# Fourier stage two with the last tokens' high and low rows in one block, and one group for two batches' middle feature

## The chip, the cores and the metric

The kernel runs on one core of a Trainium2 chip. Its engines work at the same time, each through its own queue in order: TensorE (PE in the rows, with PEld for the loading of the stationary operand), VectorE (DVE), ScalarE (ACT), GpSimd (POOL) and SyncE (SP), which here only issues transfers. The metric is the device time of the one launch in microseconds (us).

## What is computed

The reference is attention with a threshold under the row maximum, then a Fourier mixing over tokens and features with a two-layer MLP, then a gated projection:

```
scores = (q @ k^T) / 8;  keep scores >= max - tau;  softmax;  attn = softmax @ v     # 4 x 8 heads x 576 x 64
x = attn as (4, 576, 512)
u = x + real(fft over features(fft over tokens(x)))                                  # "mixed"
un = (u - mean) / sqrt(var + 1e-6)
y = u + relu(un @ w_ch1) @ w_ch2                                                     # 512 -> 2048 -> 512
out = (sigmoid(conv of 5 tokens of y) * (y @ w_val)) @ w_out
```

The change touches only `mixed`. Since x is real, the real part of the two-dimensional transform needs cosine sums and sine sums alone, over the even and the odd part of x in the tokens. Stage one sums over features, stage two over tokens.

## The kernel before

**Numbers in two parts.** A matrix product with nearly float32 accuracy is made from float32r operands split into a rounded high part and the low rest: high x high, low x high and high x low, three matmuls that add into one PSUM tile. Names end in `h` and `l` for the two.

**Stages.** Attention goes pair of heads by pair (16 pairs, `p`), nine tiles of 128 query rows each (144 tiles, `g_tile`). For each tile: PE makes the scores `s` (line 667), DVE takes their maximum `neg` (L732), ACT makes `e` = exp (L738), DVE masks and sums into `p` (L749), POOL divides (L757), PE transposes into `t` (L769), ACT copies to `m` (L786), and later PE multiplies by v (L447). There are two PSUM tiles for scores, so tile g waits for L749 of tile g-2. Four pairs are a batch; after a batch's last pair comes its Fourier part `g_fft(b)`. Beside all this the MLP's weights, which arrive as float64 words, are converted in 32 pieces (`Wide.stages`, L278 to L288: five steps on DVE, two or three on ACT, one on POOL). When the last scores are done, PSUM is given to the MLP, whose chunk 0 (512 tokens) is woven with the rest of the Fourier part (`g_h` L1239, `g_c` L1275). Chunks 1 to 4 (L1085, L1101) and the gated output (L1473, L1491) follow in an order written out in the code.

**Fourier stage one** (`g_fft`, L566). The folded tokens (289 cosine rows, 287 sine rows) are cut into three blocks of 97, 96, 96 and 96, 96, 95 (`E_BLK`, `O_BLK`). A group for one block is 8 matmuls (cosine, 258 columns) or 6 (sine, 256 columns). `g_parts` then takes it out of PSUM: ACT writes the high part (`aeh`, `boh`, L540) and DVE the low rest (`ael`, `bol`, L550); in the last batch ACT makes a second copy and POOL the subtraction (L547).

**Fourier stage two** (`stage2`, L579). For each of two feature blocks `j` there is a cosine and a sine group of 128 features by 290 tokens, 9 matmuls each: three products times three token blocks. Ahead of them a group of 9 makes the middle feature (row 256, two columns of `aeh`) of this batch, which ACT copies to `ny` (L592) and then into row 0 of `dd` and `sm` (L618, L620). DVE makes `dd` = `ws` - f and `sm` = `ws` + f (L605, L607), POOL adds them to the tokens, and SP stores the result `u_d`. So stage two is 45 matmuls a batch, 180 in all; stage one is 168.

**What sets the order.** All work up to the end of chunk 0 is placed by `Loom`: a list planner that runs when the kernel is built, with an estimate for every step, ranks and due times (`rank`, `due`, `SPREAD`, `FFT_LATE`), and constants that say how far a low-ranked step may go ahead (`NEAR`, `HOLD`) and what a change of work on PE costs (`SWAP`, `FILL`, `STAY`). `DICE` seeds small random shifts in its choices. What comes out is a fixed order for each engine. The order from the first matmul of chunk 1 on does not come from these constants.

Of the kernel before, what the change touches and what calls it, by code (L numbers as in the profile page):

```python
# [29 lines left out]
CE = DM // 2 + 2  # L30
KE = HALF + 2
E_BLK = [(0, 97), (97, 96), (193, 96)]
O_BLK = [(1, 96), (97, 96), (193, 95)]
# [30 lines left out]
def f32(ap):  # L64
    return ap.bitcast(F32)
# [251 lines left out]
def attention_fft(tc, right, ps_f, a, u_d, dram, conv_w, loom):  # L317
# [3 lines left out]
    with ExitStack() as right2, ExitStack() as right2b, ExitStack() as right3, ExitStack() as right4, ExitStack() as scores, ExitStack() as turned:  # L321
# [34 lines left out]
        ael = dft.tile([128, 3, CE], F32R, name="ael")  # L356
# [32 lines left out]
        def g_consts():  # L389
            for nm, shape in (("cd", [128, 2, CE]), ("sd", [128, 2, DM // 2]), ("cs", [97, 3, KE]), ("ss", [96, 3, KE])):  # L390
                for part in "hl":
                    t = dft.tile(shape, F32R, name=nm + part)
# [26 lines left out]
        NPT, FFT_OPS = 9 * NP, 87  # L419
# [49 lines left out]
        def g_fold(p):  # L469
# [24 lines left out]
            ends, inner, back = slice(0, HALF + 1, HALF), slice(1, HALF), slice(S - 1, HALF, -1)  # L494
            whole = ("DVE", dve(S), 3, "port") if p >= NPAIR - 2 else ("POOL", 1435.0, 2, "port")
            eng = DVE if p >= NPAIR - 2 else POOL

            def g_half(kind, s):
                op = ALU.subtract if kind else ALU.add
                yield "POOL", pool_ns(HALF), 2, "port"  # L500
                POOL.tensor_tensor(out=t[kind][:, inner], in0=s[:, inner], in1=s[:, back], op=op)
                yield "POOL", 290.0, 2, "port"
                POOL.tensor_copy(t[kind][:, ends], s[:, ends])
                if kind and j == 0:
                    yield "POOL", 780.0, 2, "port"
                    POOL.tensor_tensor(out=t[1][0:1, inner], in0=d[0:1, inner], in1=d[0:1, back], op=ALU.add)
# [16 lines left out]
        def g_fft(b):  # L523
            yield "after", ("folded", b * NP + NP - 1), ("cst",), *([("fft", b - 1)] if b else [])
            xs, rev = xs_d.pop(b), rev_d.pop(b)
# [6 lines left out]
            aeh, ael, boh, bol = a_b[0:2] + [fft_p.tile([128, 3, DM // 2], F32R, tag=nm, name=nm) for nm in ("boh", "bol")]  # L532

            def g_parts(kind, nb, m, n, f, room):
# [3 lines left out]
                fv, hv, lv = f[0:m, 0:n], *(x[0:m, nb, 0:n] for x in ((boh, bol) if kind else (aeh, ael)))  # L538
                yield "ACT", act(n), 0.3
                ACT.activation(hv, fv, AF.Copy)  # L540
                if b == B - 1:
                    t = fft_p.tile([128, KE], F32, tag=("ws", "sm")[nb % 2], name="sp")[0:m, 0:n]
# [4 lines left out]
                    POOL.tensor_tensor(out=lv, in0=t, in1=f32(hv), op=ALU.subtract)  # L547
                else:
                    yield "DVE", dve(n), 0.25
                    DVE.tensor_tensor(out=lv, in0=fv, in1=f32(hv), op=ALU.subtract)  # L550
# [3 lines left out]
            for kind in range(2):  # L554
# [3 lines left out]
                for nb, (n0, m) in enumerate(O_BLK if kind else E_BLK):  # L558
# [12 lines left out]
            def stage2(odd, c0, m=128):  # L571
                hi, lo, sh, sl = (boh, bol, cst["ssh"], cst["ssl"]) if odd else (aeh, ael, cst["csh"], cst["csl"])
                i = 0
                for ww, ss in ((hi, sh), (lo, sh), (hi, sl)):
                    for nb, (_, k) in enumerate(O_BLK if odd else E_BLK):
                        yield ("PE", KE / 2.4 + 13.5, rank(), "full", *(["room"] if i == 0 else []))
                        if i == 0:
                            f, room = fill_tile()
                        PE.matmul(out=f[0:m, 0:KE], lhsT=ww[0:k, nb, c0:c0 + m], rhs=ss[0:k, nb, :], start=(i == 0), stop=(i == 8))  # L579
                        i += 1  # L580
# [9 lines left out]
            def g_ny(f, room):  # L590
# [1069 lines left out]
```

## Time and profile before

| what | us |
|---|---|
| time, median of 3 runs | 856.27 |
| lowest and highest | 854.34, 858.76 |
| the profiled execution, its own time | 852.85 |
| the profiled execution, its span | 851.1 |
| PE busy | 818.5 (96%) |
| DVE busy | 562.6 (66%) |
| ACT busy | 417.8 (49%) |
| POOL busy | 380.5 (45%) |

The span runs from the first to the last instruction; 1.75 us of the profiled execution lie around it. Busy time is the share in which an engine has an instruction in work. Matmuls overlap in the pipeline, so the time of one matmul is read from the distance between starts, not from its duration. The span falls into three stretches: attention up to the last scores at 306.15 us, the rest of the planned part with chunk 0 to the first matmul of chunk 1 at 433.27 us, and the remainder.

### The profile page before, as it was taken

What the parts mean: (1) busy time and instruction counts of PE and PEld (TensorE: products, weight loads), DVE (VectorE), ACT (ScalarE), POOL (GpSimd) and SP (SyncE); (2) the same over time, 40 slices, a digit from 0 to 9 for tenths busy, and PEclk for the clock granted to TensorE, in tenths of its full rate; (3) what the DMA queues carried; (4) which work ended last, traced back from release to release, by engine and by line L of the source; (5) the groups of instructions that cost most, each with busy time, mean ns of one, the idle gap of its engine ahead of it and who ended that gap; (6) DMA issues with size and microseconds to landing.
All of it is one profiled execution on the core that took longest, in us unless ns stands there. A gap on an engine that the chain in (4) does not pass through costs nothing.

```text
span 851.1 us, 13928 instructions
## 1 busy us (share of the span) xinstructions
PE 818.5 (96%) x4920; PEld 653.6 (77%) x4920; DVE 562.6 (66%) x1212; ACT 417.8 (49%) x855; POOL 380.5 (45%) x450
## 2 busy tenths in 40 slices
PE   7889999989999998999999999999999999999997
PEld 5555556656665666888899999998888788889986
DVE  6999999999899999897747542142123756329730
ACT  4777786777778774744535222133121331143432
POOL 4546965687668755675353331022003010085421
PEclk9999999999999999999999999999999999999999
DMA  6357444426553559966945621013000230532111
GB/s 214 106 172 237 121 133 155 155 104 221 191 183 107 191 195 378 343 219 222 383 154 170 202 88 38 1 39 98 1 1 24 82 106 1 198 130 82 62 50 62
DMA packets 64765, 119.47 MB, mean 140 GB/s; under 512 B 14514, under 2 KB 21682, under 8 KB 64696
## 3 DMA queue, kind: packets, MB, share of 16 engines
q1 hardware_dynamic: 57448, 95.01, 32.4%
q0 software_dynamic: 7104, 23.57, 9.1%
q8 instruction: 39, 0.64, 0.3%
q14 instruction: 30, 0.25, 0.1%
q10 hardware_dynamic: 144, 0.00, 0.0%
HBM read 87.09 MB, written 31.47 MB: 139 GB/s over the span
## 4 chain that ended last, share of the span: by engine, by line
PE 63%; DVE 16%; ACT 7%; POOL 5%; issue 5%; DMA 3%; SPq 0%; DVEq 0%; POOLq 0%; ACTq 0%
PE c L1101 16%; PE h L1085 16%; DVE p L749 5%; PE o L1491 5%; DVE neg L732 5%; PE c L1275 5%; PE v L1473 5%; PE h L1239 4%; PE s L667 4%; ACT e L738 4%; PE f L447 2%; ACT m L786 2%; PE t L769 2%; POOL p L757 2%; PE f L579 2%
## 5 line engine op out<-in xcount | busy, mean ns | idle before, releaser
L757 POOL TENSOR_SCALAR p<-p,su 128x576 f32<-128x576 f32 x144 | 109.0, 766 | 92.1 <-DVE su L684 84.2
L1089 DVE SCALAR_TENSOR_TENSOR hl<-h,hh 128x384 fp32r<-128x384 f32 (+1 forms) x64 | 39.9, 623 | 147.8 <-ACT hh L1088 147.8
L1088 ACT ACTIVATE hh<-h 128x384 fp32r<-128x384 f32 (+1 forms) x64 | 34.8, 544 | 203.7 <-PE h L1085 198.5
L738 ACT ACTIVATE e<-s,neg 128x576 f32<-128x576 f32 x144 | 104.7, 742 | 53.7 <-DVE neg L732 39.2
L749 DVE SCALAR_TENSOR_TENSOR p<-s,thr,e 128x576 f32<-128x576 f32 x144 | 114.4, 816 | 16.7 <-ACT e L738 7.9
L732 DVE TENSOR_REDUCE neg<-s 128x1 f32<-128x576 f32 x144 | 103.3, 748 | 5.7 <-PE s L667 5.0
L667 PE MATMUL s<-kt,qt 64*128 64x288 f32 (+1 forms) x640 | 97.5, 437 | 9.6 <-DVE p L749 8.5
L1101 PE MATMUL c<-hl,w1h 128*128 128x384 f32 (+1 forms) x256 | 93.0, 363 | 0.1
L1101 PE MATMUL c<-hh,w1l 128*128 128x384 f32 (+1 forms) x256 | 92.6, 362 | 0.0
L1101 PE MATMUL c<-hh,w1h 128*128 128x384 f32 (+1 forms) x256 | 92.6, 362 | 0.0
L769 PE MATMUL t<-ident,p 128*128 128x128 f32 x496 | 75.3, 280 | 11.1 <-ACT m L786 5.9
L667 PEld LDWEIGHTS s<-kt,qt 64*128 64x128 f32 (+1 forms) x640 | 45.5, 174 | 47.7 <-issue 12.3
L769 PEld LDWEIGHTS t<-ident,p 128*128 128x128 f32 x496 | 53.8, 141 | 35.6 <-POOL p L757 17.1
L786 ACT ACTIVATE m<-t 128x512 f32<-128x512 f32 x124 | 72.0, 600 | 3.0 <-PE t L769 2.9
L447 PE MATMUL f<-m,v 128*64 128x320 f32 (+1 forms) x512 | 69.6, 411 | 0.3 <-ACT th L704 0.3
L1085 PE MATMUL h<-unh,w0h 128*128 128x384 f32 (+1 forms) x256 | 61.6, 362 | 0.0
L1085 PE MATMUL h<-unh,w0l 128*128 128x384 f32 (+1 forms) x256 | 61.6, 362 | 0.0
L1085 PE MATMUL h<-unl,w0h 128*128 128x384 f32 (+1 forms) x256 | 61.6, 362 | 0.0
L1110 POOL TENSOR_TENSOR res<-ht,res 128x512 f32<-128x512 f32 (+1 forms) x20 | 23.0, 1186 | 84.5 <-DVE ht L1109 84.5
L447 PEld LDWEIGHTS f<-m,v 128*64 128x64 f32 x512 | 33.7, 137 | 27.2 <-issue 4.4
L1101 PEld LDWEIGHTS c<-hl,w1h 128*128 128x128 f32 x256 | 48.1, 188 | 6.1 <-DVE hl L1089 1.2
L1101 PEld LDWEIGHTS c<-hh,w1l 128*128 128x128 f32 x256 | 48.1, 188 | 5.0
(264 smaller groups left out, 1705.4 us busy)
## 6 DMA issues: line engine op xcount, KB each, us to landing
raw<-in_moe_w_ch POOLq DMA_DIRECT2D x32, 512.0 KB, 6.4
qt<-in_q SPq DMA_DIRECT2D x15, 576.0 KB, 5.2
kt<-in_k SPq DMA_DIRECT2D x15, 432.0 KB, 3.5
ypad<-y_d SPq DMA_DIRECT2D x16, 288.0 KB, 2.9
out<-os SPq DMA_DIRECT2D x18, 256.0 KB, 2.0
v<-in_v SPq DMA_DIRECT2D x16, 256.0 KB, 3.2
e_h<-cx SPq DMA_DIRECT2D x16, 256.0 KB, 3.8
e_l<-ct SPq DMA_DIRECT2D x16, 256.0 KB, 4.2
```

Of the source, the lines that this page charges most:

```text
L447: PE.matmul(out=f[h * 64:h * 64 + 64, 0:n], lhsT=w, rhs=r, start=(t == 0), stop=(t == 4))
L667: PE.matmul(out=s[o, c, 0:HALF], lhsT=qt[w, hh, q], rhs=kt[w, 2 if h == 2 and hh else hh], start=True, stop=True)
L732: DVE.tensor_reduce(out=neg[u][:, j, 0:1], in_=sc[g][:, :, 0:HALF], axis=AX.XY, op=ALU.max, negate=True)
L738: ACT.activation(e, sc[g][:, :, 0:HALF], AF.Exp, bias=neg[u][:, j, 0:1], scale=1.0)
L749: DVE.scalar_tensor_tensor(out=p_view(g).rearrange("p (a b) -> p a b", a=2), in0=sc.pop(g)[:, :, 0:HALF], scalar=thr[u][:, j:j + 1], in1=e ...
L757: POOL.tensor_scalar(out=v, in0=v, scalar1=ssum[u][:, j:j + 1], scalar2=1.0, op0=ALU.mult, op1=ALU.mult)
L769: PE.matmul(out=f[:, t, :], lhsT=pv[:, t * 128:(t + 1) * 128], rhs=ident, is_transpose=True, start=(t == 0), stop=(t == 3))
L786: ACT.activation(o, fv, AF.Copy)
L1085: PE.matmul(out=f[:, 0:n], lhsT=ww[:, k * 128:(k + 1) * 128], rhs=x[:, k, 0:n], start=(i == 0), stop=(i == 3 * KB - 1))
L1101: PE.matmul(out=ch[c][o][:, 0:n], lhsT=ww[:, o * 128:(o + 1) * 128], rhs=x, start=(at_ == 0 and i == 0), stop=(at_ == FB - 1 and i == 2))
L1275: PE.matmul(out=ch[0][o][:, 0:n], lhsT=ww[:, o * 128:(o + 1) * 128], rhs=x, start=(j == 0 and i == 0), stop=(j == FB - 1 and i == 2))
L1473: PE.matmul(out=f[:, 0:HALF], lhsT=w[:, k, o * 128:(o + 1) * 128], rhs=x[:, k, s], start=(i == 0), stop=(i == 3 * KB - 1))
```

## The change

**Packed last block.** The 289 cosine rows are put in another order: tokens 1 to 287, then 0 and 288. The folded sums are written at offset 0 (`most`) with the two end tokens behind (`two`). Blocks are now 128, 128 and 33 rows (cosine) or 31 (sine). In the third block the high part goes to rows 0 and up, the low rest to rows 64 and up of the same tile (`h[LOW:LOW + m]`), and for the sine a second copy of the high part to rows 32 and up. The constants `csh` and `ssh` hold matching rows in their third block. One matmul with 97 or 95 rows then does what three did. For the cosine the product of the high part with the low constants is a second matmul with 33 rows. A cosine group is 8 matmuls instead of 9, a sine group 7.

**Tile shape.** The program that is built gives the 33-row matmuls of stage two a TensorE tile of 64 rows, the shape that the scores have; the stage-one groups of 33 and 31 output rows get tiles of 64 and 32 columns. Before, all Fourier matmuls had the full tile, apart from the two-column groups of the middle feature, with 32 columns.

**Evacuation of the third block.** DVE does the subtraction in all four batches; for the sine ACT does one more copy. The last batch's second copy on ACT and its subtraction on POOL go for these blocks.

**One group for two batches' middle feature.** Stage one now makes feature 256 twice, ahead of features 0 to 255 and behind them. Even batches write columns 0 to 256 of `aeh`, odd ones 1 to 257, so that column 0 keeps the even batch's middle feature while column 257 takes the odd batch's. One group of 8 in every second batch then makes both. `g_ny` adds them to the two token rows with two DVE operations reading PSUM, and SP stores two single rows. The two copies into `dd` and `sm` go, and the store of `xr` for j = 0 has 127 rows. Chunk 0's load now also waits for batch 1's group.

Stage two has 136 matmuls instead of 180.

**Planner constants.** Several of them and the seeds change, so the order of the planned part is another one throughout. From the first matmul of chunk 1 on, the order on every engine is the same as before.

```diff
-E_BLK = [(0, 97), (97, 96), (193, 96)]
-O_BLK = [(1, 96), (97, 96), (193, 95)]
+NB = 2
+REST = HALF + 1 - NB * 128
+LOW = 64
-HOLD = {"PE": 200.0, "DVE": 200.0, "ACT": 200.0, "POOL": 200.0}
-NEAR = 20.0
+HOLD = {"PE": 200.0, "DVE": 200.0, "ACT": 100.0, "POOL": 350.0}
+NEAR = 120.0
-SPREAD = 26
-FFT_LATE = 2
+SPREAD = 32
+FFT_LATE = 6
-RANK = {"D": 1, "A": 1, "P": 2.5}
+RANK = {"D": 2.5, "A": 9, "P": 2.5}
-SWAP = 450.0
-FILL = 200.0
-STAY = 80.0
+SWAP = 350.0
+FILL = 100.0
+STAY = 160.0
...
             def g_parts(kind, nb, m, n, f, room):
...
-                fv, hv, lv = f[0:m, 0:n], *(x[0:m, nb, 0:n] for x in ((boh, bol) if kind else (aeh, ael)))
+                h, l = (boh, bol) if kind else (aeh, ael)
+                v = slice(0, n) if kind else slice(b % 2, b % 2 + DM // 2 + 1)
+                hv, fv = h[0:m, nb, v], f[0:m, v]
                 yield "ACT", act(n), 0.3
                 ACT.activation(hv, fv, AF.Copy)
-                if b == B - 1:
+                if nb == NB:
+                    yield "DVE", dve(n), 0.25
+                    DVE.tensor_tensor(out=h[LOW:LOW + m, nb, v], in0=fv, in1=f32(hv), op=ALU.subtract)
+                    if kind:
+                        yield "ACT", act(n), 0.3
+                        ACT.activation(h[32:32 + m, nb, v], fv, AF.Copy)
+                    loom.free(room)
+                elif b == B - 1:
...
-            def stage2(odd, c0, m=128):
+            def stage2(odd, c):
                 hi, lo, sh, sl = (boh, bol, cst["ssh"], cst["ssl"]) if odd else (aeh, ael, cst["csh"], cst["csl"])
+                ops = [(ww, ss, nb, 128) for ww, ss in ((hi, sh), (lo, sh), (hi, sl)) for nb in range(NB)] + [(hi, sh, NB, LOW + REST - 2 * odd)]
+                if not odd:
+                    ops.append((hi, sl, NB, REST))
...
-            def g_ny(f, room):
-                yield "ACT", act(KE), 0.3
-                ACT.activation(ny, f[0:1, 0:KE], AF.Copy)
+            def g_ny(f, room, x):
+                up, dn, md = slice(0, HALF + 1), slice(S - 1, HALF, -1), slice(1, HALF)
+                yield "DVE", dve(KE), 0.25
+                DVE.tensor_tensor(out=x[:, up], in0=x[:, up], in1=f[0:2, up], op=ALU.add)
+                yield "DVE", dve(KE), 0.25
+                DVE.tensor_tensor(out=x[:, dn], in0=x[:, dn], in1=f[0:2, md], op=ALU.add)
                 loom.free(room)
+                for i in range(2):
+                    SP.dma_start(out=u_d[b - 1 + i][DM // 2:DM // 2 + 1], in_=x[i:i + 1])
...
         def g_first():
-            yield "after", ("added", 0, 0), ("added", 0, 1), ("s", LEFT)
+            yield "after", ("added", 0, 0), ("added", 0, 1), ("ny", 1), ("s", LEFT)
```

How the order moves is shown at two places, both on PE. The first is the start of stage one for batch 0, which lies in pair 6. In the rows, `s` is scores, `t` and `f<-ident,p` transposes, `f<-cdh,xeh` and the like stage one. Before:

```order
L667 MATMUL s<-kt,qt 128x288 x4
L769 MATMUL t<-ident,p 128x128 x4
L566 MATMUL f<-cdh,xeh 97x258 x2
L769 MATMUL t<-ident,p 128x128 x4
L566 MATMUL f<-cdh,xel 97x258 x2
L566 MATMUL f<-cdl,xeh 97x258
L769 MATMUL f<-ident,p 128x128 x4
L566 MATMUL f<-cdl,xeh 97x258
L566 MATMUL f<-od,xoh 97x258
L566 MATMUL f<-od,xol 97x258
L769 MATMUL t<-ident,p 128x128 x4
L667 MATMUL s<-kt,qt 128x288 x4
```

And now, from the scores to the end of the first two groups (the other four groups follow before the next scores):

```order
L686 MATMUL s<-kt,qt 128x288 x4
L788 MATMUL t<-ident,p 128x128 x4
L583 MATMUL f<-cdh,xeh 128x258 x2
L583 MATMUL f<-cdh,xel 128x258 x2
L583 MATMUL f<-cdl,xeh 128x258 x2
L583 MATMUL f<-od,xoh 128x258
L583 MATMUL f<-od,xol 128x258
L583 MATMUL f<-cdh,xeh 128x258 x2
...
L788 MATMUL t<-ident,p 128x128 x8
```

Between two scores there stood one group of 8 in pieces; now all six groups, 42 matmuls, stand between two scores.

The second place is PE behind the last scores, where `f<-m` and `f<-th` are the products with v and `h` is chunk 0's first layer. Before, the rest of batch 2's stage one and all of its stage two stood there:

```order
L667 MATMUL s<-kt,qt 64x288 x4
L694 MATMUL f<-ident,p 128x128 x2
L566 MATMUL f<-cdh,xeh 96x258 x2
L769 MATMUL t<-ident,p 128x128 x4
L566 MATMUL f<-cdh,xel 96x258 x2
L566 MATMUL f<-cdl,xeh 96x258 x2
...
L447 MATMUL f<-th_256_197,vt_194 64x256 x2
L579 MATMUL f<-csh,aeh 2x290 x3
L579 MATMUL f<-csh,ael 2x290 x3
```

Now:

```order
L686 MATMUL s<-kt,qt 64x288 x4
L717 MATMUL f<-ident,p 64x64 x2
L455 MATMUL f<-m_3863,v_193 64x256 x8
L455 MATMUL f<-th_256_197,vt_194 64x256 x2
L788 MATMUL t<-ident,p 128x128 x8
...
L455 MATMUL f<-m_4164,v_195 64x320 x8
L455 MATMUL f<-th_320_200,vt_196 64x320 x2
L1258 MATMUL h<-unh,w0h_4213 128x512 x4
```

Batch 2's Fourier part has moved ahead of the last scores, and only the transposes and the products with v stand between them and chunk 0.

## Rows read from the trace of the kernel before

**Rows 1.** The page, slices: busy tenths of PE and DVE, PE's granted clock.

```profile
PE   7889999989999998999999999999999999999997
...
DVE  6999999999899999897747542142123756329730
...
PEclk9999999999999999999999999999999999999999
```

**Rows 2.** Busy time by stretch: length, then PE, PEld, DVE, ACT, POOL, clock, DMA.

```profile
0.00:306.15 306.15, 283.06 (x2120) 182.63 (x2120) 275.11 (x678) 226.47 (x492) 202.82 (x267) 1.00 0.51 165
306.15:433.27 127.12, 122.88 (x655) 99.91 (x651) 105.80 (x171) 68.78 (x137) 72.19 (x81) 1.00 0.78 277
433.27:851.10 417.83, 412.57 (x2151) 371.08 (x2149) 181.66 (x364) 122.59 (x227) 105.49 (x103) 1.00 0.24 81
```

**Rows 3.** Timeline of PE: start, us, line, shape (rows*columns of the stationary operand), count.

```profile
309.00 0.40 PE L566 MATMUL f<-sdh,xoh 128*96 128x256 f32 x2
309.24 0.40 PE L566 MATMUL f<-sdh,xol 128*96 128x256 f32 x2
...
366.52 1.07 PE L1239 MATMUL h<-unh,w0h 128*128 128x512 f32 x4
367.42 0.57 PE L579 MATMUL f<-csh,aeh 97*2 97x290 f32 x3
367.83 0.57 PE L579 MATMUL f<-csh,ael 97*2 97x290 f32 x3
368.23 1.09 PE L1239 MATMUL h<-unh,w0l 128*128 128x512 f32 x4
```

**Rows 4.** Timeline of PE around the last scores.

```profile
304.61 0.28 PE L566 MATMUL f<-od,xol 128*96 128x258 f32 x1
304.82 1.40 PE L667 MATMUL s<-kt,qt 64*128 64x288 f32 x12
306.15 0.44 PE L694 MATMUL f<-ident,p 128*128 128x128 f32 x2
```

**Rows 5.** Waits of DVE up to 309 us: total, times, longest.

```profile
DVE p L749 <- ACT e L738: 7.9, 24, 0.9
DVE neg L732 <- PE s L667: 5.0, 19, 0.5
```

**Rows 6.** Waits of PE from 306.15 to 433.27 us.

```profile
PE c L1275 <- DVE hl L1253: 2.8, 1, 2.8
PE f L566 <- DVE ael L550: 0.8, 2, 0.6
```

**Rows 7.** Groups of DVE up to 435 us: busy us, mean ns.

```profile
L283 DVE SCALAR_TENSOR_TENSOR raw<-raw,ct 128x512 f32<-128x512 uint32 x32 | 26.9, 842 | 0.5 <-ACT ct L281 0.5
L282 DVE SCALAR_TENSOR_TENSOR cx<-raw,cx 128x512 int32<-128x512 int32 x32 | 24.6, 767 | 1.8 <-ACT cx L280 1.8
L278 DVE TENSOR_SCALAR cx<-raw 128x512 int32<-128x512 int32 x32 | 22.5, 705 | 0.0
...
L284 DVE TENSOR_SCALAR raw<-cx 128x512 int32<-128x512 int32 x32 | 16.8, 525 | 0.0
...
L284 DVE TENSOR_SCALAR cw_raw<-cw_x 128x20 int32<-128x20 int32 x1 | 4.8, 4827 | 0.0
...
L1119 DVE TENSOR_TENSOR z<-z,cs 128x512 f32<-128x512 f32 (+1 forms) x8 | 4.5, 612 | 0.0
L550 DVE TENSOR_TENSOR ael<-f,aeh 96x258 fp32r<-96x258 f32 (+1 forms) x9 | 3.8, 421 | 0.3 <-ACT aeh L540 0.2
...
L605 DVE TENSOR_TENSOR dd<-ws,f 128x290 f32<-128x290 f32 x7 | 3.1, 448 | 2.0 <-PE f L579 2.0
...
L282 DVE SCALAR_TENSOR_TENSOR cw_x<-cw_raw,cw_x 128x20 int32<-128x20 int32 x1 | 0.8, 777 | 0.0
```

**Rows 8.** Last weight pieces (POOL) and chunk 0's last first-layer step (PE).

```profile
421.93 1.15 POOL L288 TENSOR_TENSOR w0l<-raw 128x512 fp32r<-128x512 f32 x1 [0.97 <-DVE raw L284]
...
424.43 1.07 PE L1239 MATMUL h<-unh,w0h 128*128 128x512 f32 x4
```

More of the change, by code (lines that the diff above doesn't have):

```diff
@@ L355, in attention_fft @@
         aeh = dft.tile([128, 3, CE], F32R, name="aeh")
-        ael = dft.tile([128, 3, CE], F32R, name="ael")
+        ael = dft.tile([128, NB, CE], F32R, name="ael")
+        boh = dft.tile([128, 3, DM // 2], F32R, name="boh")
+        bol = dft.tile([128, NB, DM // 2], F32R, name="bol")
+        for t in (aeh, boh):
+            DVE.memset(f32(t[0:LOW, NB]), 0.0)
         NPAIR = B * NP
@@ L494, in g_fold @@
             ends, inner, back = slice(0, HALF + 1, HALF), slice(1, HALF), slice(S - 1, HALF, -1)
+            most, two = slice(0, HALF - 1), slice(HALF - 1, HALF + 1)
             whole = ("DVE", dve(S), 3, "port") if p >= NPAIR - 2 else ("POOL", 1435.0, 2, "port")
@@ L500, in g_half @@
                 yield "POOL", pool_ns(HALF), 2, "port"
-                POOL.tensor_tensor(out=t[kind][:, inner], in0=s[:, inner], in1=s[:, back], op=op)
+                POOL.tensor_tensor(out=t[kind][:, most], in0=s[:, inner], in1=s[:, back], op=op)
                 yield "POOL", 290.0, 2, "port"
-                POOL.tensor_copy(t[kind][:, ends], s[:, ends])
+                POOL.tensor_copy(t[kind][:, two], s[:, ends])
                 if kind and j == 0:
                     yield "POOL", 780.0, 2, "port"
-                    POOL.tensor_tensor(out=t[1][0:1, inner], in0=d[0:1, inner], in1=d[0:1, back], op=ALU.add)
+                    POOL.tensor_tensor(out=t[1][0:1, most], in0=d[0:1, inner], in1=d[0:1, back], op=ALU.add)
                 h, l = (q[:, j, 0:HALF + 1] for q in fold[b][kind])
@@ L557, in g_fft @@
                 n = DM // 2 if kind else CE
-                for nb, (n0, m) in enumerate(O_BLK if kind else E_BLK):
+                for nb in range(NB + 1):
+                    n0, m = nb * 128, 128 if nb < NB else REST - 2 * kind
                     ops = [(xx[:, j, n0:n0 + m], dd[:, j, 0:n]) for xx, dd in ((xh, dh), (xl, dh), (xh, dl)) for j in range(2)]
@@ L569, in g_fft @@
             loom.mark("spent", b)
-            def stage2(odd, c0, m=128):
+            def stage2(odd, c):
                 hi, lo, sh, sl = (boh, bol, cst["ssh"], cst["ssl"]) if odd else (aeh, ael, cst["csh"], cst["csl"])
[L573 to L580, printed above, removed]
+                ops = [(ww, ss, nb, 128) for ww, ss in ((hi, sh), (lo, sh), (hi, sl)) for nb in range(NB)] + [(hi, sh, NB, LOW + REST - 2 * odd)]
+                if not odd:
+                    ops.append((hi, sl, NB, REST))
+                for i, (ww, ss, nb, k) in enumerate(ops):
+                    yield ("PE", KE / 2.4 + 13.5, rank(), "full", *(["room"] if i == 0 else []))
+                    if i == 0:
+                        f, room = fill_tile()
+                    w = ww[0:k, nb, c]
+                    PE.matmul(out=f[0:w.shape[-1], 0:KE], lhsT=w, rhs=ss[0:k, nb], start=(i == 0), stop=(i == len(ops) - 1))
                 return f, room
@@ L637, in g_fft @@
                 SP.dma_start(out=xr, in_=rev[j * 128:(j + 1) * 128])
-                if j == 0:
-                    ny = fft_p.tile([1, KE], F32, tag="ny", name="ny")
-                    f, room = yield from stage2(False, DM // 2, CE - DM // 2)
-                    loom.add(g_ny(f, room))
-                f, room = yield from stage2(False, j * 128)
+                if b % 2 and j == 0:
+                    ny = fft_p.tile([2, S], F32, tag="ny", name="ny")
+                    for i, t in enumerate((ny_d, rev)):
+                        SP.dma_start(out=ny[i:i + 1], in_=t[0:1])
+                    f, room = yield from stage2(False, slice(0, CE, CE - 1))
+                    loom.add(g_ny(f, room, ny))
+                f, room = yield from stage2(False, slice(1 + j * 128, 129 + j * 128))
                 loom.add(g_even(j, f, room, ws))
-                f, room = yield from stage2(True, j * 128)
+                f, room = yield from stage2(True, slice(j * 128, j * 128 + 128))
                 loom.add(g_odd(j, f, room, x, xr, ws, dd, sm))
             loom.mark("fft", b)
-        a_b = [aeh, ael]
         tiles = []
@@ L788, in g_tile @@
             loom.mark("mc", g)
[L790 removed]
+        idle = fft_p.tile([128, S], F32, tag="diff", name="idle")[:, 0:128]
         DVE.memset(idle, 0.0)
```

56 lines of the change are left out of this document (28 added, 28 removed), and 6 rows, old and new, of the table DICE.

## The prediction

> **What bounds the kernel now.** I read the slices of the page first: PE is busy in nine tenths or more of nearly every slice from end to end, at a granted clock of full speed (2.4 GHz), while DVE is as full as PE in the first 16 slices and much emptier in the second half [rows 1]. So the profile has two regimes, and busy time by stretch shows where they meet [rows 2]. Up to the last scores (306.15 us) PE is busy for 283.06 us and DVE for 275.11 us: 23.1 and 31.0 us idle, neither clearly the bound. From there to the first matmul of chunk 1 (433.27 us) PE has 122.88 of 127.12 us. After that it has 412.57 of 417.83 us. Work taken off PE is worth its full time in the second stretch; in the first it is worth something only if DVE allows. The third stretch has the same instructions in the same order on every engine before and after, so I carry its 417.8 us over. It starts when chunk 0 is done, so all that is gained or lost is what happens to 433.27 us.
>
> The waits say how the engines are bound together in the first stretch. DVE waits 7.9 us for ACT's exp and 5.0 us for scores [rows 5]; this is the loop of tiles itself, and the remaining 18 us of DVE's idle time are the start and spots where nothing was placed.
>
> **What a matmul costs.** A group of three stage-two matmuls starts 0.41 and 0.40 us after the one ahead (367.42, 367.83, 368.23): 0.135 us each, with 290 columns, although it has 97 rows and only two output columns [rows 3]. Two stage-one matmuls take 0.24 us, so 0.12 each [rows 3]. 180 - 136 = 44 stage-two matmuls go: 44 x 0.135 = 5.9 us of PE. Stage one keeps its 168. That each block now has 128 rows instead of 96 costs nothing by the same rows, since a two-column group and a 128-column group keep the same pace.
>
> **Tile shapes, an added cost.** Ten matmuls have 33 rows and a 64-row tile (8 in the cosine groups, 2 in the middle feature's). No Fourier matmul of before has such a tile; the nearest are the scores. The last matmul ahead of them starts at 304.61 and should hand over after 0.12 us, at 304.73; the scores start at 304.82, so 0.09 us are lost, and perhaps as much on the way out [rows 4]. The two-column group, whose tile is narrow too but has full rows, loses nothing on either side: 0.90 us behind an h group of 4, and 0.40 to the next [rows 3]. So a visit to the 64-row tile costs between 0 and 0.18 us, ten visits between 0 and 1.8 us; I take half, 0.9 us, because the shape is that of the scores and the number type that of the other row. The eight stage-one groups with narrow output have the tile kind of the two-column group, so I take nothing; by the price of the scores it would be 8 x 0.18 = 1.4 us at most. Net on PE: 5.9 - 0.9 = 5.0 us less.
>
> **The second stretch.** Where the last scores stand, the changed order has 42 stage-one and 38 stage-two matmuls still to do, against 68 and 90. So 26 x 0.12 + 52 x 0.135 = 10.1 us leave this stretch; 44 matmuls of that are the saving and 34 are moved ahead. The stretch also had a stall of 2.8 us: c waited for `hl` [rows 6]. `hl` stood on DVE behind a step on 20 elements of the conv weights that took 4.83 us [rows 7]. The changed order has that step at tile 96, inside attention, so the stall goes. What is late next is the drain of attention: the last transposes wait for the last tiles to be masked and divided, and two products with v now stand there in place of stage one. I add 0.6 us for a wait there, the longest that stage one had in the same drain [rows 6], and 0.3 for three row-tile visits. 127.1 - 10.1 - 2.8 + 0.9 = 115.1 us. Bounds: 114.2 without added waits; 118.5 if a stall of the old size comes back.
>
> Can the weights follow? POOL finishes the piece for chunk 0's last h at 423.1, and this h starts at 424.43: 1.35 us to spare [rows 8]. When the last tile is masked, 12 of the 32 pieces were finished on DVE, and 13 are in the changed order: 20 in 127.1 us before, 19 in 115 now, 6.4 and 6.1 us for each. DVE's work in the stretch falls from 105.8 us by the 10.9 that move out and rises by 2.6 (both below), to 97.5 of 115 [rows 2]. The share is about the same, so I charge nothing; if the cover fails it is a few tenths for each late piece.
>
> **The first stretch.** PE gets 34 matmuls (26 stage one, 8 stage two): 3.1 + 1.1 us, and seven row-tile visits, 0.6 us. DVE gets, counted in the two orders up to the last L749 and priced by [rows 7]: one more first step of a weight piece (0.71), two L282 (1.53), one L283 (0.84), one L284 (0.53), the conv weights' steps (1.3, and 0.4 or 4.8 for the long one), two L1119 (1.22), four evacuations (4 x 0.42), four of the `dd`/`sm` kind (4 x 0.45), and two for the middle feature by the same row (0.9): 10.9 us, or 15.3 with the long step. That is more than PE's 4.8 us. Over the whole planned part DVE's own increase is small: two more evacuations and four middle-feature steps, 6 x 0.44 = 2.6 us; the rest is work pulled ahead. ACT loses 10 instructions in all, POOL two; both have a third or a quarter of the stretch free [rows 2], so I cost these at nothing.
>
> How long does the stretch get? If the extra work all fits into idle time: 306.2. If PE keeps its 23.1 us idle: 283.1 + 4.8 + 23.1 = 311.0. If DVE keeps its 31.0: 275.1 + 10.9 + 31.0 = 317.0. I take 312.5, nearer to PE's, because the changed order puts Fourier work in blocks between two scores, where DVE is idle for want of scores, and it is there that the conversions were put.
>
> The other moves cost nothing I can see: the single-row stores and loads are short, and chunk 0's load has the rest of attention to wait in.
>
> **Sum.** 312.5 + 115.1 + 417.8 = 845.4 us of span, 5.7 less than 851.1. The profiled execution took 852.85, so 847.1; it stands 3.4 below the median of the runs, and against this median I forecast 856.27 - 5.7 = **850.6 us**.
>
> **Rivals.**
>
> *DVE is the bound of attention.* DVE keeps its idle time: 317.0 + 115.1 + 417.8 = 849.9, 1.2 us less, **855.1**. For it: DVE's work is within 8 us of PE's there, and its waits are loop waits [rows 2, 5]. Against: 18 us of its idle time are none of those. With the long conv-weight step it is +3.2, 859.5.
>
> *The pulled work hides entirely.* 306.2 + 115.1 + 417.8 = 839.1, 12.0 us less, **844.3**. For it: both engines have over 20 us idle. Against: it would ask PE to lose a fifth of its idle time and DVE a third.
>
> *Row tiles cost more.* All twenty passages and the sixteen of the narrow groups at the scores' price: 3.2 instead of 0.9 us, so 3.4 us less, **852.9**. The rows leave this open: the scores lose 0.09 us on entry [rows 4], the two-column group nothing [rows 3]. The Trainium skill, "TensorEngine Tiling (Array Packing)", section Key Properties, says that changing the tiling mode drains the engine; by that rule every one of the 36 passages would cost, those of the narrow groups too, and this rival would be the forecast. The two-column rows of this trace do not show such a loss.
>
> *Blocks of stage one hold up the scores: slower.* All six groups of a batch now stand between two scores, and PE takes them in order. Each needs one of two PSUM tiles, free only when ACT and DVE have emptied it; DVE has `neg` and `p` queued ahead, and behind the waiting group stand the scores that DVE needs next. The trace has two such waits, 0.8 us together [rows 6]. Three batches have 18 groups. On top of a DVE-bound attention, 18 waits of 0.6 us (the longest of the two) add 10.8 us: 851.1 - 1.2 + 10.8 = 860.7, **865.9**. It turns from no change to slower where the mean wait exceeds (1.2 + 4.3) / 18 = 0.31 us. Against: between the second and third and the fourth and fifth group stand 8 or more transposes, 0.7 us in which a tile can be emptied.
>
> That the change doesn't save its matmuls is excluded by the count in the order.
>
> **Chances.** Forecast 0.46, hidden entirely 0.12, DVE-bound 0.20, row tiles 0.10, slower 0.12. A measurement of this kernel can tell about 0.5% from no change, 4.3 us: faster is below 852.0, slower above 860.6. Of the forecast's 0.46 some 0.40 lie below 852.0; with 0.12 and 0.03 of the row tiles, faster has 0.55. Same: 0.06 + 0.20 + 0.07 = 0.33. Slower: 0.12. The range goes from just below the hidden case, 843, to where the DVE-bound case with its long step ends, 859.
>
> **What would show it.** Right: PE busy some 5 us less over the span; stage-two starts still 0.135 apart; last scores at 311 to 314 us; first matmul of chunk 1 at 427 to 428; no wait of c for `hl` near the start of chunk 0; the third stretch 417.8. Wrong: last scores at 317 or later with DVE idle still 31 us (DVE-bound), waits of stage-one groups for DVE or ACT in attention (blocks), gaps over 0.1 us around the 33-row matmuls (row tiles), or waits of h for POOL late in chunk 0 (weights).

## The result and the profile after

| | before | after |
|---|---|---|
| median of 17 runs each | 855.49 us | 859.82 us |
| profiled execution | 852.85 us | 858.65 us |
| its span | 851.1 us | 856.9 us |
| last scores done (the next PE instruction starts) | 306.15 us | 317.07 us |
| first matmul of chunk 1 | 433.27 us | 439.10 us |

The changed kernel takes 1.0053 times as long (95% interval 1.0041 to 1.0065). It was forecast at 850.6, 0.7% faster. 859.8 lies 0.8 us above the upper end of the range.

The page's slices, against [rows 1]: PE is still busy almost everywhere, but the row of its granted clock is no longer full throughout.

```profile
PE   8999999999889997999999999999999999999997
...
PEclk9999999999999998999999999999999999999999
```

The three stretches, which answer [rows 2] (length, then busy time of PE, PEld, DVE, ACT, POOL, granted clock, DMA share, GB/s):

```profile
0.00:317.07 317.07, 290.00 (x2154) 188.75 (x2155) 284.52 (x704) 234.17 (x502) 210.28 (x276) 0.99 0.50 163
317.07:439.10 122.03, 115.11 (x578) 91.56 (x575) 94.97 (x153) 61.17 (x116) 64.36 (x71) 0.97 0.75 266
439.10:856.90 417.80, 412.51 (x2151) 370.96 (x2149) 182.18 (x364) 122.67 (x227) 105.45 (x103) 1.00 0.24 81
```

The third stretch has not moved (417.80). Attention is 10.9 us longer, where 6.4 were forecast; the second stretch is 5.1 us shorter, where 12.0 were forecast. So 4.6 us are missing in the first and 6.9 in the second. Each loss has one wait at its centre. PE's busy time over the span is 817.6 us, 0.9 less than before, where some 5 less were forecast; a lower clock makes the same work longer.

**The wait in the second stretch.** PE's timeline in chunk 0 (start, us, line, shape, count, and in brackets the idle time before and what ended it):

```profile
333.06 1.07 PE L1258 MATMUL h<-unl,w0h 128*128 128x512 f32 x4
339.12 2.08 PE L1258 MATMUL h<-unh,w0h 128*128 128x512 f32 x4 [4.99 <-DMA w0h<-e_h]
340.99 1.91 PE L1258 MATMUL h<-unh,w0l 128*128 128x512 f32 x4
342.69 1.34 PE L1258 MATMUL h<-unl,w0h 128*128 128x512 f32 x4
343.87 0.39 PE L1294 MATMUL c<-hh,w1h 128*128 128x512 f32 x1
```

The second `h` waits 4.99 us for its weights, which come back from DRAM. And it is slow afterwards: its 12 matmuls take 4.75 us (339.12 to 343.87), where the same 12 take 2.74 us at full clock (334.08 to 336.82 in e1, below). The windows show why (length, busy times and clock as above):

```profile
330.00:338.00 8.00, 4.13 (x22) 2.54 (x18) 7.47 (x9) 4.58 (x9) 6.21 (x8) 0.90 1.04 403
338.00:342.00 4.00, 2.88 (x7) 2.33 (x8) 0.00 (x0) 0.00 (x0) 1.24 (x3) 0.50 1.06 392
342.00:346.00 4.00, 4.00 (x17) 3.24 (x16) 1.30 (x2) 0.93 (x2) 0.80 (x1) 0.85 1.04 397
```

After the idle time the granted clock is 0.50, the 1.2 GHz level, and then comes back. Wait and low clock make 5.0 + 2.0 = 7.0 us, and 6.9 were missing.

Why were the weights late? SP's timeline holds the cause, a long way ahead of the wait:

```profile
303.31 0.24 SPq L643 DMA_DIRECT2D u_d<-xr  x1
303.99 4.35 SPq L654 DMA_DIRECT2D xd<-xs  x1
317.14 0.32 SPq L655 DMA_DIRECT2D xr<-xr  x1
...
323.56 0.43 SPq L929 DMA_DIRECT2D w0h<-e_h  x1
...
329.75 0.58 SPq L929 DMA_DIRECT2D w0h<-e_h  x1
```

SP issues nothing between 308.3 and 317.1 us. Then come the load of `v`, the mirrors, stores and only at 323.56 the first weights of chunk 0, for the first `h`; those for the second `h` follow at 329.75. In the kernel before, the first were issued ahead of the last scores:

```profile
302.67 0.43 SPq L910 DMA_DIRECT2D w0h<-e_h  x1
```

The waits of SP up to 445 us (total, times, longest) say what it stood at:

```profile
SPq L655 <- DMA u_d<-xr: 26.6, 3, 9.1
```

and in the kernel before, at the same load:

```profile
SPq L637 <- DMA u_d<-xr: 10.6, 3, 5.1
```

Three times, once for each of batches 0 to 2, the load of `xr` for the second half waits some 9 us (3.5 before) for the store of `xr` of the first half, whose buffer it takes. That store is L643, and for the first half the change made it `xr[r:]` with `r` = 1: 127 rows. What the DMA engines moved while it ran is in the data rate between 309 and 314 us, in 40 slices:

```profile
GB/s 203 147 129 74 37 276 350 406 424 295 74 18 37 18 37 18 18 37 18 37 18 18 37 18 37 18 18 37 18 18 37 18 37 18 18 37 18 37 18 18
```

Once the other transfers are done, 18 to 37 GB/s are left, where all engines together reach 424 in this row. A slice is 0.125 us, in which 18 GB/s are one row of 2304 B and 37 are two. From 303.31 to 317.14, where SP goes on, the store's 286 KB take 13.8 us, 21 GB/s; a sixteenth of 424 would be 26.5. In the kernel before, the store had 128 rows and landed 2.6 us after its issue (median of seven, from its page of DMA issues):

```profile
u_d<-xr SPq DMA_DIRECT2D x7, 288.0 KB, 2.6
```

The Trainium skill, "DMA: Bandwidth & Descriptors", section "Why a DMA increments its semaphore by 16 and not by 1", says under "How many engines" that a transfer runs on the largest number of engines up to 16 that divides its row count, and gives 127 rows as a case that runs on one. The trace agrees with it: from 313 to 316 us, with little else under way, the mean busy share of the 16 DMA engines was 0.08, and one engine alone would be 0.06.

**The wait in attention.** DVE's timeline of batch 1's middle feature:

```profile
216.64 0.45 DVE L611 TENSOR_TENSOR ny<-ny,f 2x289 f32<-2x289 f32 x1 [3.44 <-PE f L455]
217.01 0.14 DVE L703 RECIPROCAL su<-su 128x2 f32<-128x2 f32 x1
...
217.44 0.74 DVE L751 TENSOR_REDUCE neg<-s 128x1 f32<-128x576 f32 x1
```

DVE stands still for 3.44 us ahead of `ny`. The releaser named is PE, but PE's middle-feature group had ended by 211.41. SP's rows show what came last: the two one-row loads of `ny`, issued at 211.63 behind 576 KB.

```profile
210.65 0.42 SPq L654 DMA_DIRECT2D xd<-xs  x1
211.13 0.46 SPq L655 DMA_DIRECT2D xr<-xr  x1
211.63 0.58 SPq L659 DMA_DIRECT2D ny<-xr  x2
```

Behind `ny` stood the reciprocal and `neg`, so exp, mask and the next scores were late too. PE then waited 3.11 us (PE's timeline):

```profile
220.15 2.14 PE L686 MATMUL s<-kt,qt 64*128 64x288 f32 x8 [3.11 <-DVE p L768]
```

and its clock fell (windows):

```profile
215.00:220.00 5.00, 2.03 (x16) 0.84 (x12) 3.19 (x10) 1.40 (x2) 1.99 (x3) 1.00 0.15 30
220.00:225.00 5.00, 4.85 (x26) 3.66 (x26) 4.66 (x12) 2.77 (x6) 1.46 (x2) 0.66 0.99 354
```

### The profile page after: what moved, and what is told of

Its sections match the earlier page's. It is cut to its first block, busy times and chain, and to the rows that moved or that the text cites. A ratio compares the mean times of both kernels' runs of the same rounds, so it can differ in the third digit from the quotient of the medians.

```text
span 856.9 us, 13836 instructions
## 1 busy us (share of the span) xinstructions
PE 817.6 (95%) x4878; PEld 651.3 (76%) x4878; DVE 561.7 (66%) x1220; ACT 418.0 (49%) x845; POOL 380.1 (44%) x448
## 4 chain that ended last, share of the span: by engine, by line
PE 70%; DVE 15%; ACT 5%; issue 5%; POOL 3%; DMA 2%; SPq 0%; DVEq 0%; ACTq 0%; POOLq 0%
PE c L1120 16%; PE h L1104 16%; DVE neg L751 6%; PE s L686 5%; PE f L455 5%; PE o L1510 5%; PE h L1258 5%; PE v L1492 5%; PE c L1294 4%; DVE p L768 4%; PE t L788 3%; ACT e L757 2%; PE f L598 2%; PE f L583 1%; DMA w0h<-e_h 1%
## 5 line engine op out<-in xcount | busy, mean ns | idle before, releaser
L757 ACT ACTIVATE e<-s,neg 128x576 f32<-128x576 f32 x144 | 102.2, 742 | 53.9 <-DVE neg L751 47.9
L768 DVE SCALAR_TENSOR_TENSOR p<-s,thr,e 128x576 f32<-128x576 f32 x144 | 112.2, 815 | 8.4 <-POOL p L776 0.2
L788 PE MATMUL t<-ident,p 128*128 128x128 f32 x464 | 69.3, 282 | 13.8 <-ACT m L805 9.8
L788 PEld LDWEIGHTS t<-ident,p 128*128 128x128 f32 x464 | 50.9, 142 | 36.3 <-issue 17.4
L805 ACT ACTIVATE m<-t 128x512 f32<-128x512 f32 x116 | 66.0, 599 | 1.1 <-PE t L788 0.6
```

What stands on the lines that cost most here:

```text
L757: ACT.activation(e, sc[g][:, :, 0:HALF], AF.Exp, bias=neg[u][:, j, 0:1], scale=1.0)
L768: DVE.scalar_tensor_tensor(out=p_view(g).rearrange("p (a b) -> p a b", a=2), in0=sc.pop(g)[:, :, 0:HALF], scalar=thr[u][:, j:j + 1], in1=e ...
L788: PE.matmul(out=f[:, t, :], lhsT=pv[:, t * 128:(t + 1) * 128], rhs=ident, is_transpose=True, start=(t == 0), stop=(t == 3))
L805: ACT.activation(o, fv, AF.Copy)
```

## The experiments

All ratios are to the kernel before, with 95% intervals; medians are of 4 to 12 runs, those of the changed kernel of 17. The kernel before was timed beside each set of runs, with medians from 854.65 to 856.01 us, so a difference between two rows read from the ratios can be about 1 us off the one read from the medians.

| run | us | ratio |
|---|---|---|
| the changed kernel | 859.82 | 1.0053 (1.0041 to 1.0065) |
| e1, store in 112 + 15 rows | 851.1 | 0.9944 (0.9922 to 0.9965) |
| e7, store in 126 + 1 rows | 850.77 | 0.9946 (0.9927 to 0.9966) |
| e2, `ny` loaded early | 856.88 | 1.0009 (0.9993 to 1.0024) |
| e3, 97 rows for 33 | 859.93 | 1.0042 (1.0028 to 1.0056) |
| e5, e1 and e2 | 847.77 | 0.9919 (0.9902 to 0.9936) |
| e6, e1, e2 and e3 | 846.66 | 0.9908 (0.9892 to 0.9923) |
| e10, e6 with 44 matmuls again | 850.72 | 0.9946 (0.9929 to 0.9962) |
| e4, before with 127 + 1 rows | 882.12 | 1.0308 (1.0283 to 1.0332) |
| e11, before with 112 + 15 + 1 rows | 854.63 | 0.9993 (0.9974 to 1.0012) |
| e8, before with the new planner numbers | 862.62 | 1.0084 (1.0059 to 1.0109) |
| e9, e5 with the old planner numbers | 866.7 | 1.0134 (1.0113 to 1.0155) |

### The store of 127 rows

**e1** cuts the store in the changed kernel:

```diff
-                r = int(j == 0)
-                SP.dma_start(out=u_d[b][DM // 2 + 128 * j + r:DM // 2 + 128 * j + 128], in_=xr[r:])
+                for lo, hi in ((1, 113), (113, 128)) if j == 0 else ((0, 128),):
+                    SP.dma_start(out=u_d[b][DM // 2 + 128 * j + lo:DM // 2 + 128 * j + hi], in_=xr[lo:hi])
```

> The changed kernel; only the store of 127 rows (xr without its first row, once a batch) is cut into two stores, of 112 and of 15 rows. Same bytes, same order of every other instruction. Theory S (the store of 127 rows is what holds up SP: issued at 303.31 us in the changed kernel, the load xr<-xr behind it waited until 317.14 us, 8.7 us of that for u_d<-xr, and the weights of chunk 0 stand behind that load): the store lands within 4 us, SP goes on, the weights for chunk 0 are asked for before 325 us, the wait of 5.0 us of h for w0h<-e_h goes, and with it the half clock after it (2.0 us): 859.8 - 7 = 853 us, ratio to the kernel before 0.995 to 0.999. Rival T (batch 2's stage two was the cover of the reload and has moved away; the DMA engines are saturated from 330 us on, whoever issues): h still waits 3 us or more, 858 to 860 us. Rival D (attention is bound by DVE): the last scores stay at 315.7 us, which S leaves open too, and the second stretch alone decides.

Measured: 851.1 us, 8.7 less than the changed kernel (theory S had said 853). SP's timeline now goes on after the store (its issue, and what followed):

```profile
304.37 0.80 SPq L643 DMA_DIRECT2D u_d<-xr  x2
305.26 0.39 SPq L654 DMA_DIRECT2D xd<-xs  x1
308.75 0.34 SPq L655 DMA_DIRECT2D xr<-xr  x1
...
316.81 0.43 SPq L929 DMA_DIRECT2D w0h<-e_h  x1
...
326.66 0.44 SPq L929 DMA_DIRECT2D w0h<-e_h  x1
```

and the second `h` follows the first without a gap, at full clock (PE's timeline):

```profile
333.16 1.08 PE L1258 MATMUL h<-unl,w0h 128*128 128x512 f32 x4
334.08 1.07 PE L1258 MATMUL h<-unh,w0h 128*128 128x512 f32 x4
...
336.82 0.39 PE L1294 MATMUL c<-hh,w1h 128*128 128x512 f32 x1
```

The last scores started at 316.77 us, 1.0 later than in the changed kernel (315.74), and chunk 1 at 431.99, 7.1 earlier. All of the gain is in the second stretch: 113.9 us from the end of the last scores, where the changed kernel took 122.0. Theory S holds. Rival T, that the moved stage two had been the cover and the engines were full anyway, is out: from 330 to 350 us the DMA share was 1.03 in this run and 1.04 in the changed kernel, but the weights for the second `h` were asked for 3.1 us earlier (326.66 against 329.75).

**e4** and **e11** put the same store into the kernel before, alone. e4:

```diff
-                SP.dma_start(out=u_d[b][DM // 2 + 128 * j:DM // 2 + 128 * j + 128], in_=xr)
+                cuts = (1, 128) if j == 0 else (0, 128)
+                SP.dma_start(out=u_d[b][DM // 2 + 128 * j + cuts[0]:DM // 2 + 128 * j + 128], in_=xr[cuts[0]:])
+                if j == 0:
+                    SP.dma_start(out=u_d[b][DM // 2:DM // 2 + 1], in_=xr[0:1])
```

e11 has three stores instead, of rows 1 to 112, 113 to 127, and 0.

> The kernel before; only its store of xr with j = 0 is cut into rows 1 to 127 and row 0, as the changed kernel has the first of them. Theory S: each such store takes 10 us or more, SP waits as long at the load xr<-xr behind it, and what is queued behind (weights, keys, the store of converted weights) comes as much later. In the kernel before the last of these in attention's wake stands at 316 us, in front of stores e_h, e_l and further weights, and PE has Fourier work there: between 1 and 6 us slower, 856.5 to 861.5. Rival T (the store does nothing by itself): 855.5, same as before.

> The kernel before, with its store of xr for j = 0 cut into 112, 15 and 1 rows: the same bytes as in the run with 127 and 1 rows, one store more. Theory S (the 27 us of that run are the 127 rows on one DMA engine): no change from the kernel before, within 1 us. Rival (three stores where there was one, or rows that start at the second partition, cost it): 870 us or more.

Measured: 882.12 us with 127 rows, 26 more than before, and 854.63 with the same bytes in three stores, no change. My bound for e4 (1 to 6 us) was far too low. I had thought of what is queued on SP alone; POOL pays more. Its timeline in e4, behind batch 0's store of 198.52 us:

```profile
216.87 0.79 POOL L611 TENSOR_TENSOR xd<-xd,dd 128x289 f32<-128x289 f32 x1 [7.31 <-DMA xd<-xs]
...
220.87 1.47 POOL L760 TENSOR_SCALAR p<-p,su 128x576 f32<-128x576 f32 x2
```

and PE's:

```profile
221.67 1.11 PE L772 MATMUL t<-ident,p 128*128 128x128 f32 x4 [8.40 <-POOL p L760]
```

POOL has the add of `xd` queued ahead of the division of the next tiles. It waits for the late load, the division waits behind it, and PE waits 8.40 us for the division. POOL stands so at the add of `xd` once in each of the batches 0 to 2 (7.3, 8.7 and 8.6 us). PE's waits up to 445 us:

```profile
PE t L772 <- POOL p L760: 16.7, 8, 8.4
PE f L566 <- POOL xel L511: 6.2, 1, 6.2
```

The first is 3.0 us in the kernel before, and the second isn't there. So 19.9 of the 26 us are waits for POOL; in the rest the lower clock has a part (0.98 over this execution, 1.00 before). In the changed kernel the order lets POOL come to batch 2's second half later:

```profile
318.00 0.80 POOL L634 TENSOR_TENSOR xd<-xd,dd 128x289 f32<-128x289 f32 x1 [0.49 <-DMA xd<-xs]
```

The load that this add waited for 0.49 us had been issued by 308.34, and it came in only 0.9 us after SP went on from the store. In e4 the add starts 0.7 us after SP goes on, all three times (216.87 after 216.16, 314.07 after 313.39, 372.35 after 371.67). So the load ends with the store, as if a part of it stood behind the store on the one engine; no run shows that directly. In the changed kernel the price on POOL hardly arose, and the weights behind SP were hit. The same store costs 8.7 us in one order and 26 in the other.

**e7** changes the size by one row, 126 and 1 in place of 112 and 15.

> The changed kernel with the store of 127 rows cut into 126 and 1 instead of 112 and 15. Theory K (the Trainium skill, DMA: Bandwidth & Descriptors, section Why a DMA increments its semaphore by 16 and not by 1, under How many engines: the transfer runs on the largest number of engines up to 16 that divides its row count; 126 has 14, 127 has 1): the store lands within a few us and the time is that of the cut into 112 and 15, 851 us. Rival M (a store is quick only if it has a multiple of 16 rows): 126 rows are as slow as 127, SP waits 9 us again for u_d<-xr, and the time stays at 858 to 861 us.

Measured: 850.77 us, the same as with 112 and 15. SP's waits for `u_d<-xr` up to 445 us in e1:

```profile
SPq L655 <- DMA u_d<-xr: 6.0, 3, 2.9
```

and in e7:

```profile
SPq L655 <- DMA u_d<-xr: 7.8, 5, 3.4
```

126 rows are quick and 127 are not, so it is no matter of multiples of 16, of the start at the second row or of fewer rows than partitions. That fits the rule of the Trainium skill on divisors, cited above (14 engines for 126, one for 127); no other row count was tried.

### The one-row loads of ny

**e2** issues them at the start of the batch's Fourier part:

```diff
             xs, rev, ny_d = xs_d.pop(b), rev_d[b], rev_d.get(b - 1)
+            if b % 2:
+                ny = fft_p.tile([2, S], F32, tag="ny", name="ny")
+                for i, t in enumerate((ny_d, rev)):
+                    SP.dma_start(out=ny[i:i + 1], in_=t[0:1])
...
                 if b % 2 and j == 0:
-                    ny = fft_p.tile([2, S], F32, tag="ny", name="ny")
-                    for i, t in enumerate((ny_d, rev)):
-                        SP.dma_start(out=ny[i:i + 1], in_=t[0:1])
```

> The changed kernel; only the two one-row loads of ny are issued at the start of the Fourier part of their batch instead of in front of its stage two, some 10 us earlier. Theory N (DVE stood 3.4 us at ny for these loads, with neg and the reciprocal behind it, and PE then waited 3.1 us for p and ran at a granted clock of 0.66 for a stretch): the wait is gone, the last scores start 4 to 5 us earlier than 315.7, and the time is 859.8 - 4.5 = 855.3 us. Rival D (DVE's work bounds attention at 317 us; the wait only takes the place of idle time that would come later): the wait is gone but the last scores move by less than 1.5 us, 858.5 to 859.8 us.

Measured: 856.88 us, 2.9 less than the changed kernel. DVE does not wait at `ny` (DVE's timeline), and the last scores start at 312.39 us, 3.35 earlier than in the changed kernel (PE's):

```profile
213.35 0.44 DVE L614 TENSOR_TENSOR ny<-ny,f 2x289 f32<-2x289 f32 x1
...
312.39 1.40 PE L686 MATMUL s<-kt,qt 64*128 64x288 f32 x12
```

Theory N holds, with 3.4 us where I had said 4 to 5. Rival D, which said that DVE-bound attention would swallow it, is out: DVE has the same work and the stretch is shorter by the length of the wait. The wait for weights differs from that of the changed kernel too (2.1 us in the profiled execution, at 852.78 the fastest of twelve that reach up to 858.06), so the time alone would not have told.

### Both mends, and the row tiles

**e3** takes 97 rows instead of 33 in ten matmuls, with zeros for the rest; **e5** is e1 and e2 together, **e6** all three.

```diff
-                    ops.append((hi, sl, NB, REST))
+                    ops.append((hi, sl, NB, LOW + REST))
```

> The changed kernel; the ten matmuls of 33 rows take 97 rows instead (the added rows of csl are zero), so that they have the tile of the matmuls around them. Same count, same order. Theory R (each visit to the 64-row tile costs the 0.18 us that the gaps on both sides show): the gaps of 0.09 us go, ten visits give back 1.8 us at most, of which some lies in attention beside DVE: 858.0 to 859.0 us. Rival: the gaps have another cause or lie where PE waits anyway: within 0.4 us of 859.8.

> The changed kernel with both mends: the store of 127 rows cut into 112 and 15, and the one-row loads of ny issued at the start of their batch's Fourier part. Theory S + N (two separate faults of the change, one behind SP, one in front of DVE): the last scores come as in the run with ny alone (312.4 us, against 316.8 with the store alone), the second stretch as in the run with the store alone (113.9 us): span 313.7 + 113.9 + 417.8 = 845.4, time 847.2, ratio to the kernel before 0.988 to 0.992. Rival (the wait at ny only takes the place of DVE's idle time once SP is free): 850 to 851, as with the store alone.

> The run before this with 97 rows instead of 33 in the ten matmuls. Theory R (the visits to the 64-row tile cost PE up to 1.8 us, which was hidden behind other waits in the first test): 0.8 to 1.8 us below the run with both mends. Rival (they lie where PE waits anyway, or the time that they take is smaller than the gaps say): within 0.4 us of it.

In the changed kernel the gaps at the 33-row matmul are there, 0.23 and 0.22 us from start to start; in e3 they are 0.13 and 0.14, the pace of the others. PE's timeline of the changed kernel:

```profile
210.89 0.30 PE L598 MATMUL f<-csh,aeh 97*2 97x290 f32 x1
211.12 0.29 PE L598 MATMUL f<-csl,aeh 33*2 33x290 f32 x1
211.34 0.53 PE L598 MATMUL f<-csh,aeh 128*128 128x290 f32 x2
```

and of e3:

```profile
212.70 0.30 PE L598 MATMUL f<-csh,aeh 97*2 97x290 f32 x1
212.83 0.30 PE L598 MATMUL f<-csl,aeh 97*2 97x290 f32 x1
212.97 0.43 PE L598 MATMUL f<-csh,aeh 128*128 128x290 f32 x2
```

The time of e3 is that of the changed kernel, 859.93, as the rival said. Without the two waits the gaps show in the time: e6 is 1.1 us below e5 (846.25 to 847.54 against 847.62 to 847.90). Ten visits to the 64-row tile cost 0.11 us each on average. For 64-row tiles this bears out the direction of the rule of the Trainium skill that the prediction cites ("TensorEngine Tiling (Array Packing)", Key Properties). For the two-column groups the trace does not show it: they keep their pace here too (0.27 for two).

e5 took 847.77 us, with 847.2 expected: the two faults are separate and their gains add up (8.7 and 2.9 us alone, about 12 together). e6 is the best version, 0.92% below the kernel before. Its stretches:

```profile
0.00:313.82 313.82, 287.26 (x2154) 187.78 (x2154) 285.01 (x704) 233.82 (x502) 209.76 (x276) 1.00 0.52 169
313.82:427.47 113.65, 112.09 (x579) 90.10 (x575) 92.96 (x153) 61.51 (x116) 65.23 (x71) 1.00 0.76 273
```

### Packing or order?

**e10** gives e6 the 44 saved matmuls back, as repeats of a group's first matmul in the same place (`more` is 1 in a cosine group, 2 in a sine group, 10 in a middle-feature group).

```diff
...
-                    PE.matmul(out=f[0:w.shape[-1], 0:KE], lhsT=w, rhs=ss[0:k, nb], start=(i == 0), stop=(i == len(ops) - 1))
+                    for x in range(1 if i else 1 + more):
+                        PE.matmul(out=f[0:w.shape[-1], 0:KE], lhsT=w, rhs=ss[0:k, nb], start=(i == 0), stop=(i == len(ops) - 1 or x < more and i == 0))
...
```

> The run with both mends and 97 rows, with the first matmul of each stage-two group issued again: 1 more in each cosine group, 2 in each sine group, 10 in each of the two middle-feature groups, 44 in all, which are the matmuls that the packing saved. The order of everything else is the same, and what is computed too. Theory P (PE's time is the bound, so each of the 44 is worth its 0.135 us): 846.7 + 5.9 = 852.6 us, the same within 0.5 as the kernel before less 2 us. Rival O (most of them lie in attention, where PE waits for DVE and ACT anyway; the gain over the kernel before is in the order): 847.5 to 850 us.

Measured: 850.72 us, 4.1 more than e6, between the two theories. The stretches say where:

```profile
0.00:315.69 315.69, 290.47 (x2182) 190.98 (x2182) 284.56 (x704) 234.11 (x502) 210.53 (x276) 1.00 0.51 168
315.69:431.99 116.30, 114.07 (x595) 91.72 (x591) 92.81 (x153) 61.16 (x116) 64.01 (x71) 1.00 0.76 267
```

The matmul counts against e6 are 28 more in attention and 16 more behind it. The 16 cost 2.65 us, 1.98 of it in PE's busy time (2.2 at 0.135 each); the rest is idle time, with a wait of 1.0 us of `h` for weights that e6 does not have. The 28 cost 1.87 of 3.8, half. So of the 8.0 us that e6 gains on the kernel before (846.66 against 854.65), 4.1 are the 44 matmuls, or 3.2 by the two ratios: about half. The other half is all else in the change, the order for the most part as I think; the new evacuation and the shared middle-feature group are in it too, and no run takes them apart.

**e8** (the kernel before with the new planner numbers) and **e9** (e5 with the old ones) were to tell the same from the other side.

```diff
-HOLD = {"PE": 200.0, "DVE": 200.0, "ACT": 200.0, "POOL": 200.0}
-NEAR = 20.0
+HOLD = {"PE": 200.0, "DVE": 200.0, "ACT": 100.0, "POOL": 350.0}
+NEAR = 120.0
...
```

(SPREAD, FFT_LATE, RANK, SWAP, FILL, STAY, DICE and the start of the planner's clock go with them; e9 is the reverse.)

> The kernel before, with the planner's numbers of the changed one and nothing else (no packing, one middle-feature group a batch, full stores): the order change alone, though the numbers were not picked for this code. 42 stage-one and 54 stage-two matmuls stand behind the last scores, against 68 and 90 in the kernel before. Theory P (what the mended change gains is the packing's matmuls, 5 us of PE, and little else): 854 to 857, no gain. Rival O (the order brings the gain, by moving batch 2's part into attention and the conv weights' step out of c's way): 848 to 851. If the numbers don't fit this code, slower than 857 is possible and says nothing on P or O.

> The changed code with both mends, with the planner's numbers of the kernel before: the packing alone, in an order near the old one (84 stage-one and 68 stage-two matmuls behind the last scores). Theory P: 5 us less than the kernel before, 850 to 851.5. Rival O: 854 to 856, since the old order leaves c waiting for hl and the Fourier work behind the last scores.

Measured: 862.62 and 866.7 us, both slower than theories P and O; for e8 the expectation had left this open. In e8 PE waits 15.6 us for `p` ahead of scores, 4.6 at the longest; in e9 the second stretch takes 137.7 us, with a wait of 4.5 us of `h` for `unl` and a granted clock of 0.83 from 330 to 350 us. The numbers belong to the code that they were picked for. Neither run separates packing from order, and nothing follows from them but that.

## Why the prediction was wrong, point by point

**The step that failed** is the sentence "the single-row stores and loads are short, and chunk 0's load has the rest of attention to wait in", under moves that cost nothing. I priced the new one-row transfers and did not price the old store that lost a row. It went from 2.6 to 13.8 us, and as SP issues in order, everything behind the next use of its buffer went with it: 8.7 us of the kernel's time by e1. No row of before shows a transfer of 127 rows, so its cost should have been bounded from both sides; with one engine of sixteen as the upper bound (286 KB at 26.5 GB/s, an estimate of 11 us from the rate row above) it would have been a rival with a place and a price.

**The loads.** They are short, as I said, but not free of the queue: 5 us from issue to use behind 576 KB. What I left out is who waits: DVE, in order, with `neg` behind it. That was 3.4 us. I counted the two `ny` steps as 0.9 us of DVE work and no wait.

**"Can the weights follow?"** I looked at the last piece in chunk 0, where it did follow (the last `h` starts at 430.94, its piece is done by 428.6). The loss was at the second `h`, at the first reloads, which I had not priced.

**The second stretch** was right otherwise: 115.1 forecast, 113.9 in e1 and 114.2 in e5. The stall of `c` for `hl` [rows 6] is gone from the waits, and the long step on the conv weights, 4.83 us before, took 0.16 at its new place. My 0.6 us for the drain came as waits of 0.43 and 0.23 us of PE for `p` in the changed kernel. The bound of 118.5 has the 0.6 twice (115.1 + 2.8 is 117.9); the measured 122.0 lies above either.

**The first stretch**: 312.5 forecast, between the bounds 311.0 and 317.0. With both mends it is 314.6 (e5), and 313.8 without row tiles (e6), 1 to 2 us more than I took: midway between the bounds, and not nearer to PE's as I had argued. The changed kernel's 317.07 equals the DVE-bound rival's 317.0 to the tenth, and DVE's idle time there, 32.6 us, is near the 31 that I had named as that rival's sign. Both are a coincidence: in e2 the same work of DVE (284.9 us busy, 284.5 in the changed kernel) fits into a stretch of 313.7 us.

**What a matmul costs.** 0.135 us each, 44 of them: 5.9 on PE. Behind the last scores they are worth that; in attention half (e10), 3.2 to 4.1 in all. **Row tiles**: 0.9 forecast for ten visits; 1.1 measured with the two waits gone (e6 against e5), nothing with them in place (e3).

**The slower rival**, blocks of stage one that hold up the scores, had the right sign and the wrong mechanism: PE's waits at stage-one groups are 0.5 us in attention and 1.0 behind it; it priced 10.8 in attention.

Forecast against the kernel before was −5.7 us. e5, the change without its two faults, is −6.9 against the kernel before timed beside it, and e6 −8.0; e5's span is 846.1 us where 845.4 was forecast. The argument on PE, DVE and the order stood within 1 to 2 us a stretch; the transfers, which I waved through, decided.

## What to carry to other kernels

Price a transfer by its row count and not by its bytes: when a diff takes one row off a 128-row store, look for what waits on its buffer and for all that is queued behind that wait on the issuing engine. A small load that an in-order engine will wait for belongs far ahead of its use, not behind the large loads of the same step. And a stall on the path costs more than its length: look at the granted clock behind it.

## What the runs showed of the hardware that I had not expected

- A store of 127 rows of 2304 B took 13.8 us at 18 to 37 GB/s; in 126 + 1 or 112 + 15 rows the longest wait of SP for it was 3.4 us. Placed in the kernel before, it cost 26 us (e4 against e11).
- While that store ran, the issue of the next load (`xd<-xs`) itself took 4.35 us instead of some 0.4 (0.39 in e1), and POOL's add waited for this load until 0.7 to 0.9 us after the store.
- After 5.0 us without work PE ran at a granted clock of 0.50 and its next 12 matmuls took 4.75 us instead of 2.7; after 3.1 us of waiting, 0.66 was the mean of the next 5 us.
